# The first transform step of two response chunks, issued behind the next pair's responses

## The chip, the cores and the metric

The kernel runs on one core of a Trainium2 chip. A core has a matrix engine (TensorE, in the profile PE for matmuls and PEld for weight loads), three engines for elementwise work (VectorE = DVE, ScalarE = ACT, GpSimd = POOL), and queues for transfers, of which SyncE's (SP) issues most. The engines work side by side and each takes its own instructions in order. TensorE writes its results to PSUM, which has eight banks per core; the other engines copy them out to SBUF.

The metric is the device time of one execution in microseconds (us), as the median of several runs. Lower is better.

## The reference

The input `x` (2048 rows of 576 columns) is normalised per row. Then three things are summed: `x` itself, a state-space convolution of the normalised rows, and a feed-forward layer (FFN) with SiLU.

```python
xn = _layernorm(x, axis=-1)
# state-space part: 576 channels with 128 modes each give a response K of 2048 steps
P = jnp.exp(logdA[:, :, None] * l[None, None, :])
K = jnp.einsum("dn,dnl,dn->dl", Cc, P, dB).real
...
y = irfft2(rfft2(up) * rfft2(Kp)) + u * Dskip      # causal convolution along 2048 rows
# FFN: 576 -> 4608 -> 576
h = _silu(jnp.einsum("bsd,df->bsf", xn, w1))
out = jnp.einsum("bsf,fd->bsd", h, w2)
return x + y + out
```

## The kernel before

Two streams are woven together. The main one is the FFN: for each of two halves of the rows, nine chunks of hidden columns, two blocks of 512 rows. `up` (lines 313 to 315) makes `ph`, 512 columns wide, from weights and rows split into a high and a low part; `down` (line 338) makes `po`, 288 columns wide, which VectorE adds to the accumulator (line 342). ScalarE and VectorE make `gf`, `gh` and `gl` from `ph` between them (lines 321 to 323).

The side stream is the convolution. Generators yield a position on the FFN's progress, and `weave` runs a side step when the FFN has come that far. The tile framework then orders the instructions of each engine with a schedule that it works out on a modelled timeline; `tc.high_priority()` puts an instruction ahead of others that are ready, and `behind(ins)` places one no earlier than behind the named instruction. So the order in which the code is written is not the order on the engines.

The change lies in `kgen`, which makes the responses. It runs over `NCK` = 36 chunks of 16 channels (8 in each half of the columns). For a chunk, ScalarE and VectorE make tables of sines and cosines `S` and `C` (lines 631 to 654). After each second chunk TensorE multiplies the tables of both:

- `kp` (line 674): 64 small products in each of two terms, with 128 rows and 32 columns of the array each, 64 columns streamed. In the trace each fp32 matmul is two instructions, so that a pair has 128 of them, 2304 in all. `behind(first)` keeps them in one run.
- `kt` (line 681): ScalarE copies the bank `kp` to SBUF.
- `z` (line 689): the first transform step of the response. Eight products with the constant `f1` and 128 columns streamed, each on one half (64 rows) of the array and into its own bank, halves taken in turn; 16 instructions in the trace, 288 in all. Each pair's first product needs `kt`.
- `stage` (line 697): ScalarE copies both banks of `z`, sorted, into a buffer that holds two pairs. When it is full, two transfers bring it to `d1k` in DRAM (line 702), 18 in all.

After the last chunk GpSimd adds the skip row to `d1k` by a transfer (line 705), and `spectral` loads it (`kr`, line 796), splits it (`kh`, `kl`, lines 790 and 791) and multiplies (`pk`, line 804).

Beside `kgen` runs `spread`, which does the same transform step for the normalised rows: `pu` (lines 155 and 156, full array, 288 columns), copied out by ScalarE (line 157, `u`) and sent to DRAM by GpSimd's queue. The two constants `s1` and `f1` come on GpSimd's queue.

`kp`, `z` and `pu` all take their banks from one pool of three, `pss`, in turn: a new tile waits until the tile three before it has been copied out. At the end of the kernel `add_conv` does the last transform step, `py` (line 825), with tiles of 64 rows and 32 columns.

Of the kernel before, what the change touches and what calls it, by code (L numbers as in the profile page):

```python
# [11 lines left out]
F32 = mybir.dt.float32  # L12
# [7 lines left out]
P = 128  # L20
# [23 lines left out]
def kernel(  # L44
# [21 lines left out]
    nc = tc.nc  # L66
# [14 lines left out]
    d1k = dram.tile([32 * P, D], F32, name="d1k")  # L81
# [9 lines left out]
    f1 = cst.tile([P, P], F32, name="f1")  # L91
# [18 lines left out]
    pss = ctx.enter_context(tc.tile_pool(name="pss", bufs=3, space=PSUM))  # L110
# [25 lines left out]
    def behind(ins):  # L136
        return tc.issue_after(ins) if ins is not None else nullcontext()
# [424 lines left out]
    def kgen():  # L562
        fT, phiT = kf["f"], kf["phi"]
        with tc.tile_pool(name="kg", bufs=1) as kg:
            CH = 8
            NRUN = 4
            NCK = HD // CH
# [32 lines left out]
            def powers(i):  # L600

                eb, wb = bases.pop(0)
                load_bases(i + 2)
                nc.scalar.copy(pw[:, :, :, :, 1].rearrange("n q (g c) k -> n q g (c k)", g=2),
                               eb.rearrange("n g q c k -> n q g (c k)"))
                pv = pw.rearrange("n r d k e -> n (r d k) e")
                R = 2 * W * 3
                nc.vector.tensor_mul(pv[:, :, 2], pv[:, :, 1], pv[:, :, 1])
                nc.vector.tensor_mul(pv[:, :, 3:5], pv[:, :, 1:3], pv[:, :, 2:3].broadcast_to([P, R, 2]))
                nc.vector.tensor_mul(pv[:, :, 5:8], pv[:, :, 1:4], pv[:, :, 4:5].broadcast_to([P, R, 3]))  # L610
                return wb

            def head(i):
                th = kg.tile([P, W, 65], F32, tag="th", name="th", bufs=2)
                nc.vector.tensor_mul(split(th), row(vt[:, 0:65], 65), col(fT, i, 65))
                with behind(pins["gl"]):
                    nc.vector.tensor_add(split(th)[:, :, :, :32], split(th)[:, :, :, :32], col(phiT, i, 32))
                return th

            stage = None  # L620
            tabs = []
            nxt = head(0)
            al = powers(0)
            for i in range(NCK):
                th = nxt
                pk, ak = pw[:, i % 2], al[:, :, i % 2]
                c65 = kg.tile([P, W, 65], F32, tag="c65", name="c65")
                S = kg.tile([P, W, 96], F32, tag="S", name="S", bufs=2)
                C = kg.tile([P, W, 96], F32, tag="C", name="C", bufs=2)
                mag = C  # L630
                nc.scalar.activation(c65, th, AF.Identity, bias=magic)  # L631
                nc.vector.scalar_tensor_tensor(th, c65, MAGIC, th, op0=ALU.subtract, op1=ALU.subtract)  # L632
                nc.scalar.activation(c65, th, AF.Abs)  # L633
                nc.scalar.activation(th, th, AF.Sin, scale=TWO_PI)
                nc.scalar.activation(c65, c65, AF.Sin, scale=-TWO_PI, bias=halfpi)
                for g in range(2):
                    gs = slice(g * CH, (g + 1) * CH)
                    nc.vector.tensor_mul(
                        mag[:, gs, 0:32].rearrange("n d (x y) -> n d x y", y=4),
                        pk[:, gs, 0, :].unsqueeze(3).broadcast_to([P, CH, 8, 4]),  # L640
                        ak[:, g].unsqueeze(2).broadcast_to([P, CH, 8, 4]))
                nc.vector.tensor_mul(
                    mag[:, :, 32:96].rearrange("n d (x y) -> n d x y", y=8),
                    pk[:, :, 1, :].unsqueeze(3).broadcast_to([P, W, 8, 8]),
                    pk[:, :, 2, :].unsqueeze(2).broadcast_to([P, W, 8, 8]))
                if i + 1 < NCK:
                    nxt = head(i + 1)
                    if i % 2 == 1:
                        al = powers(i + 1)
                for dst, t, sg in ((S, th, -1.0), (C, c65, 1.0)):  # L650
                    ov3 = dst.rearrange("n d (x y) -> n d x y", y=32)[:, :, 0:3:2, :]
                    mv3 = mag.rearrange("n d (x y) -> n d x y", y=32)[:, :, 0:3:2, :]
                    nc.vector.tensor_mul(ov3, t[:, :, 0:64].rearrange("n d (x y) -> n d x y", y=32), mv3)
                    nc.vector.scalar_tensor_tensor(dst[:, :, 32:64], t[:, :, 64:32:-1], sg, mag[:, :, 32:64],  # L654
                                                   op0=ALU.mult, op1=ALU.mult)
                tabs.append((S, C))
                if i % 2 == 0:
                    yield (i + 1) / NCK
                    continue

                kp = pss.tile([P, 512], F32, tag="pss", name="kp")
                first = None
                for e in (1, 0):
                    S, C = tabs[e]
                    for gl in range(2):
                        for gp_ in range(2):
                            o = e * 256 + (gl * 2 + gp_) * 64
                            for q in range(4):
                                ch = gp_ * CH + gl * 4 + q
                                dst = kp[32 * q:32 * q + 32, o:o + 64]  # L670
                                begins = e == 1 and gl == 0 and gp_ == 0
                                with tc.high_priority(), behind(None if begins else first):
                                    for n, t in enumerate((C, S)):
                                        mm = nc.tensor.matmul(dst, t[:, ch, :32], t[:, ch, 32:],  # L674
                                                              start=begins and n == 0, stop=True,
                                                              tile_position=(0, 32 * q), skip_group_check=True)
                                if begins:
                                    first = mm.ins
                tabs = []
                kt = kg.tile([P, 512], F32, tag="kt", name="kt")  # L680
                nc.scalar.copy(kt, kp)

                z = [pss.tile([P, 512], F32, tag="pss", name="z") for _ in range(2)]
                first = None
                for eg in range(4):
                    for h in (1, 0):
                        rows = slice(64 * h, 64 * h + 64)
                        with tc.high_priority(), behind(first):
                            mm = nc.tensor.matmul(z[h][:, eg * P:(eg + 1) * P], kt[rows, eg * P:(eg + 1) * P], f1[rows],  # L689
                                                  start=True, stop=True, tile_position=(64 * h, 0))  # L690
                        first = first or mm.ins
                r = (i - 1) % NRUN
                if r == 0:
                    stage = kg.tile([P, 64, NRUN * CH], F32, tag="stage", name="stage")
                sv = stage[:, :, r * CH:(r + 2) * CH].rearrange("p k (e h c) -> p h e k c", h=2, c=2)
                for h in range(2):
                    nc.scalar.copy(sv[:, h], z[h].rearrange("p (e k c) -> p e k c", e=4, c=2))
                if r == NRUN - 2:
                    d0 = (i // NRUN) * NRUN * CH
                    kv = d1k.rearrange("(k n) (g d) -> g n k d", n=64, g=2)  # L700
                    for gp_ in range(2):
                        nc.sync.dma_start(kv[gp_, :, :, d0:d0 + NRUN * CH], stage[gp_ * 64:(gp_ + 1) * 64])
                yield (i + 1) / NCK

        nc.gpsimd.dma_start(d1k.rearrange("(k n) d -> n k d", n=P)[0],
# [135 lines left out]
    def side():  # L841
# [3 lines left out]
        with tc.tile_pool(name="kf", bufs=1) as kfp:  # L845
# [50 lines left out]
            with tc.tile_pool(name="up", bufs=1) as up:  # L896
                sp = spread(up)
                for n, at in enumerate(kgen()):
                    if n > 1:
                        next(sp, None)  # L900
                    yield marks[0] + at * (marks[1] - marks[0])
                for _ in sp:
                    pass
# [97 lines left out]
```

## Time and profile before

| | |
|---|---|
| median of 3 runs | 1114.06 us (1113.56 to 1114.08) |
| profiled execution | 1113.42 us, of which its span is 1111.6 us |
| TensorE busy | 1103.3 us (99%), 9168 matmul instructions |
| VectorE busy | 916.9 us (82%) |
| ScalarE busy | 709.2 us (64%) |
| `kp` runs | 18, first start 170.2 us, last 640.2 us into the span |
| `z` runs | 18, first start 177.7 us, last 646.1 us |
| `kt` copies | 18 of 0.572 us (median) |
| `stage` copies | 36 of 0.644 us (median) |

The span runs from the first to the last instruction. In the views below, an instruction's row gives the start and the duration in us, the engine, the line, the operation, the output and the inputs, the tile of the array as rows*columns (only TensorE), the shapes, and how many neighbours of the same kind were merged into the row. A merged row's duration goes from the first one's start to the last one's end. Matmuls are pipelined, so that the next one starts long before the recorded end of the one before; the distance of the starts tells what an instruction costs in the stream.

### The profile page before, as it was taken

Reading aid. Unit: us, or ns where it says so; the run is one execution under the profiler, and the core shown is the slowest. Engines: PE = TensorE matmul, PEld = TensorE weight load, DVE = VectorE, ACT = ScalarE, POOL = GpSimd, SP = SyncE. Lnnn points to the kernel's source line nnn. Section 1 sums busy time; section 2 is a strip of 40 time slices with the busy share of each in tenths; the row PEclk is TensorE's granted clock in tenths of the full one; section 3 lists DMA queues with packets and bytes.
Section 4 is the critical chain, followed back from the end, with each engine's and each line's share of the span. In section 5 each row is a group of like instructions: output and inputs, shape, how many; then the busy total and the mean of one; then the engine's idle time right before and its main releaser. Section 6 shows DMA issues by size and latency. Waiting matters only on the chain.

```text
span 1111.6 us, 22913 instructions
## 1 busy us (share of the span) xinstructions
PE 1103.3 (99%) x9168; PEld 997.8 (90%) x9168; DVE 916.9 (82%) x1546; ACT 709.2 (64%) x1228; POOL 69.8 (6%) x129
## 2 busy tenths in 40 slices
PE   8999999999999999999999999999999999999998
PEld 6998999899889899899989989999999999999887
DVE  6899899999999999999999837787778778784433
ACT  5574456676777676677866536877777878773210
POOL 1100000000000000011000000000000000000111
PEclk9999999999999999999999999999999999999999
DMA  9745522425242515255844163554545445434983
GB/s 258 201 122 152 137 71 61 120 63 130 82 107 80 134 61 131 77 149 161 219 123 105 44 173 106 169 157 128 161 145 150 139 146 171 129 107 130 248 211 86
DMA packets 175563, 148.56 MB, mean 134 GB/s; under 512 B 111024, under 2 KB 142272, under 8 KB 175328
## 3 DMA queue, kind: packets, MB, share of 16 engines
q1 hardware_dynamic: 165136, 112.33, 38.7%
q0 software_dynamic: 9568, 33.62, 9.5%
q8 instruction: 72, 1.18, 0.5%
q10 hardware_dynamic: 752, 1.15, 0.4%
q14 instruction: 35, 0.29, 0.1%
HBM read 102.53 MB, written 44.61 MB: 132 GB/s over the span
## 4 chain that ended last, share of the span: by engine, by line
PE 97%; DMA 1%; DVE 0%; SPq 0%; issue 0%; ACT 0%; ACTq 0%; POOL 0%; DVEq 0%
PE po L338 42%; PE ph L313 35%; PE kp L674 3%; PE ph L314 3%; PE ph L315 3%; PE pu L804 2%; PE pb L804 2%; PE pk L804 2%; PE z L689 2%; PE pu L155 1%; DMA acc<-in_A_u_dram 1%; PE py L825 1%; PE pu L156 1%; DMA w2r<-in_B_w_dram 0%; PE pt L124 0%; DVE st L186 0%
## 5 line engine op out<-in xcount | busy, mean ns | idle before, releaser
L338 PE MATMUL po<-w2l,gh 128*128 128x288 f32 x1152 | 338.5, 295 | 0.9 <-DVE w2l L302 0.9
L338 PE MATMUL po<-w2h,gl 128*128 128x288 f32 x1152 | 336.2, 295 | 0.0
L338 PE MATMUL po<-w2h,gh 128*128 128x288 f32 x1152 | 335.8, 295 | 0.0
L338 PEld LDWEIGHTS po<-w2h,gh 128*128 128x128 f32 x1152 | 215.1, 188 | 7.6 <-issue 2.8
L338 PEld LDWEIGHTS po<-w2l,gh 128*128 128x128 f32 x1152 | 215.9, 188 | 6.1 <-DVE w2l L302 1.1
L338 PEld LDWEIGHTS po<-w2h,gl 128*128 128x128 f32 x1152 | 215.4, 188 | 0.8
L321 ACT ACTIVATE gf<-ph 128x512 f32<-128x512 f32 (+1 forms) x148 | 86.4, 585 | 142.9 <-PE ph L315 128.3
L313 PE MATMUL ph<-xh,w1h 128*128 128x512 f32 (+1 forms) x592 | 162.1, 388 | 1.2 <-ACT gf L321 1.2
L313 PE MATMUL ph<-xl,w1h 128*128 128x512 f32 (+1 forms) x592 | 161.4, 386 | 0.0
L313 PE MATMUL ph<-xh,w1l 128*128 128x512 f32 (+1 forms) x592 | 161.0, 385 | 0.0
L342 DVE TENSOR_TENSOR acc<-po,acc 128x288 f32<-128x288 f32 x288 | 126.4, 452 | 37.4 <-PE po L338 36.1
L323 DVE TENSOR_TENSOR gl<-gf,gh 128x512 fp32r<-128x512 f32 (+1 forms) x148 | 99.2, 673 | 64.8 <-ACT gh L322 64.1
L313 PEld LDWEIGHTS ph<-xh,w1l 128*128 128x128 f32 x592 | 108.1, 188 | 19.9
L313 PEld LDWEIGHTS ph<-xl,w1h 128*128 128x128 f32 x592 | 108.0, 188 | 20.0 <-DVE xl L126 0.2
L313 PEld LDWEIGHTS ph<-xh,w1h 128*128 128x128 f32 x592 | 104.5, 188 | 18.5 <-ACT gf L321 1.8
L322 ACT CAST gh<-gf 128x512 fp32r<-128x512 f32 (+1 forms) x148 | 89.8, 609 | 10.1 <-PE po L338 7.1
L631 ACT ACTIVATE c<-th,magic 128x1040 f32<-128x1040 f32 x36 | 42.1, 1169 | 37.9 <-DVE C L654 28.0
L633 ACT ACTIVATE c<-th 128x1040 f32<-128x1040 f32 x36 | 38.7, 1075 | 34.0 <-DVE th L632 34.0
L300 ACT CAST w2h<-w2r 128x576 fp32r<-128x576 f32 x72 | 46.9, 671 | 17.2 <-PE po L338 14.9
L282 DVE TENSOR_TENSOR w1l<-w1r,w1h 128x640 fp32r<-128x640 f32 x72 | 57.1, 818 | 0.2
L314 PE MATMUL ph<-x,w1h 128*128 128x512 f32 (+1 forms) x148 | 57.0, 385 | 0.0
L315 PE MATMUL ph<-x,w1l 128*128 128x512 f32 (+1 forms) x148 | 56.9, 385 | 0.0
(184 smaller groups left out, 1830.1 us busy)
## 6 DMA issues: line engine op xcount, KB each, us to landing
w2r<-in_B_w_dram SPq DMA_DIRECT2D x72, 288.0 KB, 3.7
w1r<-in_B_w_dram SPq DMA_DIRECT2D x35, 512.0 KB, 3.9
d1u<-u POOLq DMA_DIRECT2D x32, 288.0 KB, 2.6
d1k<-stage SPq DMA_DIRECT2D x18, 512.0 KB, 6.8
ur<-d1u SPq DMA_DIRECT2D x32, 288.0 KB, 3.9
kr<-d1k SPq DMA_DIRECT2D x32, 288.0 KB, 2.8
d<-yo POOLq DMA_DIRECT2D x32, 288.0 KB, 3.7
ys<-d SPq DMA_DIRECT2D x32, 288.0 KB, 11.6
```

The costliest lines, as they stand in the source:

```text
L282: pins["w1l"] = nc.vector.tensor_sub(l1, src, h1).ins
L300: pins["w2h"] = nc.scalar.copy(h2, r2).ins
L313: nc.tensor.matmul(ph, w[:, kt, :], v[:, kt, a:e], start=n + kt == 0, stop=False)
L314: nc.tensor.matmul(ph, h1[:, 4, :], x4[:, a:e], start=False, stop=False)
L315: pins["pe"] = nc.tensor.matmul(ph, l1[:, 4, :], x4[:, a:e], start=False, stop=True).ins
L321: nc.scalar.activation(gf, ph, AF.Silu)
L322: pins["gh"] = nc.scalar.copy(gh, gf).ins
L323: pins["gl"] = nc.vector.tensor_sub(gl, gf, gh).ins
L338: pins["pe"] = nc.tensor.matmul(po[:, :HD], G[blk, t][g][:, js], W2[half, c, t][w][:, hs], start=n == 0, stop=n == 3 * FT - 1).ins
L342: nc.vector.tensor_add(acc[j][:, hs], po[:, :HD], acc[j][:, hs])
L631: nc.scalar.activation(c65, th, AF.Identity, bias=magic)
L804: nc.tensor.matmul(dst, st, mv[:, hs], start=n == 0, stop=n == 3 * len(terms) - 1)
```

## The change

The `z` step of a pair moves out of the loop body into a function `along`. It is no longer issued behind its own pair's `kt`, but behind the next pair's last `kp` matmul (`mm.ins`, passed as `first`), ahead of that pair's `kt` copy. The finished `kt` tiles wait in a list `kts`; so that one can wait while the next is written, `kt` has two buffers. The pair after the last has no responses, so that the last `kt` is transformed right behind its copy, with no instruction to stand behind (`along(None)`; its first `z` then serves as `first` for the others). The copies into `stage` and the transfers to `d1k` move along with `z`. All instructions and their shapes stay.

```diff
             stage = None
+            kts = []
+
+            def along(first):
+                nonlocal stage
+                i, kt = kts.pop(0)
+                z = [pss.tile([P, 512], F32, tag="pss", name="z") for _ in range(2)]
+                for eg in range(4):
+                    for h in (1, 0):
+                        rows = slice(64 * h, 64 * h + 64)
+                        with tc.high_priority(), behind(first):
+                            mm = nc.tensor.matmul(z[h][:, eg * P:(eg + 1) * P], kt[rows, eg * P:(eg + 1) * P], f1[rows],
+                                                  start=True, stop=True, tile_position=(64 * h, 0))
+                        first = first or mm.ins
+                r = (i - 1) % NRUN
...
+                for h in range(2):
+                    nc.scalar.copy(sv[:, h], z[h].rearrange("p (e k c) -> p e k c", e=4, c=2))
+                if r == NRUN - 2:
...
+                        nc.sync.dma_start(kv[gp_, :, :, d0:d0 + NRUN * CH], stage[gp_ * 64:(gp_ + 1) * 64])
...
                 tabs = []
-                kt = kg.tile([P, 512], F32, tag="kt", name="kt")
+                if kts:
+                    along(mm.ins)
+                kt = kg.tile([P, 512], F32, tag="kt", name="kt", bufs=2)
                 nc.scalar.copy(kt, kp)
-
-                z = [pss.tile([P, 512], F32, tag="pss", name="z") for _ in range(2)]
-                first = None
-                for eg in range(4):
...
+                kts.append((i, kt))
+                if i + 1 == NCK:
+                    along(None)
                 yield (i + 1) / NCK
```

More of the change, by code (lines that the diff above doesn't have):

```diff
@@ L620, in kgen @@
             stage = None
+            kts = []
[11 more added lines that the diff above has]
+                r = (i - 1) % NRUN
+                if r == 0:
+                    stage = kg.tile([P, 64, NRUN * CH], F32, tag="stage", name="stage")
+                sv = stage[:, :, r * CH:(r + 2) * CH].rearrange("p k (e h c) -> p h e k c", h=2, c=2)
+                for h in range(2):
+                    nc.scalar.copy(sv[:, h], z[h].rearrange("p (e k c) -> p e k c", e=4, c=2))
+                if r == NRUN - 2:
+                    d0 = (i // NRUN) * NRUN * CH
+                    kv = d1k.rearrange("(k n) (g d) -> g n k d", n=64, g=2)
+                    for gp_ in range(2):
+                        nc.sync.dma_start(kv[gp_, :, :, d0:d0 + NRUN * CH], stage[gp_ * 64:(gp_ + 1) * 64])
             tabs = []
@@ L679, in kgen @@
                 tabs = []
-                kt = kg.tile([P, 512], F32, tag="kt", name="kt")
+                if kts:
+                    along(mm.ins)
+                kt = kg.tile([P, 512], F32, tag="kt", name="kt", bufs=2)
                 nc.scalar.copy(kt, kp)
-                z = [pss.tile([P, 512], F32, tag="pss", name="z") for _ in range(2)]
-                first = None
-                for eg in range(4):
[L686 to L702, printed above, removed]
+                kts.append((i, kt))
+                if i + 1 == NCK:
+                    along(None)
                 yield (i + 1) / NCK
```

## The prediction

> **What bounds the kernel now.** I read the busy times and the chain of waits first, then TensorE's own waits, then the stage that the change touches, and last the order in time at the edges of the two small runs.
>
> ```profile
> PE 1103.3 (99%) x9168; PEld 997.8 (90%) x9168; DVE 916.9 (82%) x1546; ACT 709.2 (64%) x1228; POOL 69.8 (6%) x129
> ...
> PE 97%; DMA 1%; DVE 0%; SPq 0%; issue 0%; ACT 0%; ACTq 0%; POOL 0%; DVEq 0%
> ```
>
> ```profile
> PE pz L857 <- DVE zero L852: 1.3, 1, 1.3
> PE ph L313 <- ACT gf L321: 1.2, 3, 0.5
> PE po L338 <- DVE w2l L302: 0.9, 1, 0.9
> PE pt L124 <- DVE xn L195: 0.2, 1, 0.2
> ```
>
> ```profile
> 165.00:600.00 435.00, 435.00 (x4598) 392.35 (x4598) 422.95 (x632) 305.85 (x463) 19.37 (x35) 1.00 0.42 110
> ```
>
> TensorE carries 97% of the chain and waits 3.6 us for others in the whole run. From 165 to 600 us, where the response chunks are made, it is busy 435.00 of 435.00 us at full clock, and VectorE 422.95 (behind the length stand PE, PEld, DVE, ACT and POOL), so VectorE is the next bound there. On TensorE only two things can change the time: the length of its stream, and a wait that is new. No matmul is added or removed, so the stream changes only by what it costs to pass from one kind of tile to another.
>
> **What an edge costs.** One pair of chunks, in TensorE's order of time (start, duration, count last):
>
> ```profile
> 170.01 0.29 PE L338 MATMUL po<-w2l,gh 128*128 128x288 f32 x1
> 170.23 0.34 PE L674 MATMUL kp<-C 128*32 128x64 f32 x8
> ...
> 171.98 0.31 PE L674 MATMUL kp<-S 128*32 128x64 f32 x6
> 172.22 0.54 PE L338 MATMUL po<-w2h,gl 128*128 128x288 f32 x2
> 172.60 0.29 PE L338 MATMUL po<-w2h,gh 128*128 128x288 f32 x1
> 172.73 0.29 PE L338 MATMUL po<-w2l,gh 128*128 128x288 f32 x1
> ...
> 177.15 0.39 PE L315 MATMUL ph<-x,w1l 128*128 128x512 f32 x1
> 177.37 0.39 PE L313 MATMUL ph<-xh,w1h 128*128 128x512 f32 x1
> 177.69 1.16 PE L689 MATMUL z<-f,kt 64*128 64x128 f32 x16
> 178.78 0.40 PE L155 MATMUL pu<-sp,s 128*128 128x288 f32 x1
> 179.02 0.30 PE L156 MATMUL pu<-sp,s 128*128 128x288 f32 x1
> ```
>
> Full-tile matmuls start 0.13 us apart at 288 columns (172.60 to 172.73) and 0.22 at 512 (177.15 to 177.37). So `kp` was due at 170.14 and starts at 170.23: 0.09 of drain. `z` was due at 177.59 and starts at 177.69: 0.10. Behind a run the first full matmul holds its place for 0.24 instead of 0.13 (178.78 to 179.02), and so do the two `po` at 172.22, which take 0.38 instead of 0.26: 0.11 for weights that could not be loaded ahead. The last `kp` starts at 172.07 (171.98 + 0.31, less the 0.22 that one lasts), 0.15 before the next `po`; the last `z` at 178.58 (177.69 + 1.16, less 0.27), 0.20 before `pu`. The third tile shape, of the last transform step, pays likewise:
>
> ```profile
> 1035.09 1.23 PE L825 MATMUL py<-ys,s 64*32 64x288 f32 x32
> 1036.25 0.40 PE L338 MATMUL po<-w2h,gh 128*128 128x288 f32 x1
> 1036.49 0.29 PE L338 MATMUL po<-w2l,gh 128*128 128x288 f32 x1
> ```
>
> Its last starts at 1035.92, 0.33 before the next, and that one holds its place 0.24. So each change of tile shape costs some 0.09 of drain and 0.11 of exposed load, whichever shapes meet: 0.20. A pair now makes four.
>
> **The change part by part.** In the built order of the changed kernel, 17 of the 18 response runs are followed at once by a `z` run. The first response run stands alone, and the last `z` has no later run to join.
>
> *The joins.* Each takes one full-tile stretch from between two runs: the exposed load behind `kp` (0.11) and the drain ahead of `z` (0.09 to 0.10) go. The drain from `kp` into something else stays, and `z`'s own exposed load is inside its 1.16. 17 x 0.205 = 3.5 us saved. No row shows `kp` beside `z`, so I bound it. If the join costs nothing, the second 0.20 goes as well: 0.40 each, 6.8. If the two shapes need a drain more, 0.10 is left: 1.7. I take 0.205, since three shapes show the same edge.
>
> [...]
>
> *The last `z`.* In the built order it comes in two pieces with six `po` between them: the four matmuls of one 64-row half, then those of the other. Whether halves overlap is seen in three narrow looks at the first run:
>
> ```profile
> 177.69 0.38 PE L689 MATMUL z<-f,kt 64*128 64x128 f32 x2
> 177.69 0.49 PE L689 MATMUL z<-f,kt 64*128 64x128 f32 x4
> 177.69 0.60 PE L689 MATMUL z<-f,kt 64*128 64x128 f32 x6
> ```
>
> Two more instructions, one of each half, add 0.11 together, and the first two start within 0.01: the halves run side by side. A piece of one half (8 instructions) therefore lasts about as long as both. The second piece costs drain 0.10, seven steps of 0.11 and the exposed load (0.88), 0.20 to the next start and 0.11 of load: 1.29 us lost. Its lower bound, if one half alone went twice as fast, is 0.85.
>
> *The later copies, bank and buffers.* The copy `kt` gets a second buffer, because it now waits a pair long for its use; nothing is behind that. The 36 copies into `stage` move to ScalarE's stretch behind `kt`; ScalarE is busy 305.85 of 435, so they cost nothing unless a bank is freed late (rivals). The first `z` of a run now waits for banks that the spread's `pu` held, with the whole FFN stream behind it; in the built order at least 7.4 us of FFN work (matmuls counted at 0.13 and 0.22) stand between the last `pu` and that run, so I cost it at 0. Without that cover it would cost one copy `u` (0.39, line 157 below) a run, 6.6 us.
>
> *The DMAs.* Of the 18 issues of `d1k<-stage`, all but the last two go out a pair later on SP's queue, past up to 20 other issues (weights, tables, `xr`), which they then no longer delay; those behind them wait if ScalarE's copy is late. Only the last pair is followed closely:
>
> ```profile
> 656.93 0.86 POOL L705 DMA_DIRECT2D d1k<-in_A_Dskip_dram  x1 [28.09 <-DMA d1k<-stage]
> 662.76 0.32 SPq L796 DMA_DIRECT2D kr<-d1k  x1
> 673.38 0.67 ACT L790 CAST kh<-kr 128x576 fp32r<-128x576 f32 x1
> 677.75 0.29 PE L804 MATMUL pk<-kh,mm 128*128 128x288 f32 x1
> ```
>
> ```profile
> kr<-d1k SPq DMA_DIRECT2D x32, 288.0 KB, 2.8
> ```
>
> POOL adds the skip row once `stage` has landed, the spectra's first load follows, lands 2.8 us on, and its cast starts 10.6 us after the issue: 7.8 of slack. The built order puts the last `z` behind 1.5 us more FFN work and adds a piece (1.2), so the chain starts 2.7 later: 0. Without that slack it would cost 2.7 once.
>
> *Sum*: 3.5 - 1.3 = 2.2 us off TensorE's stream. The profiled execution took 1113.42 (span 1111.6 and 1.8 around it), which gives 1111.2; the median of the runs, 0.64 above it, gives 1114.06 - 2.2 = 1111.8. About 0.2% (2.2 us) is what a measurement can tell from no change, so the sum lies on that bound.
>
> **Rivals.** *The join costs less.* If drain or load is hidden too, 0.30 a join: 5.1 - 1.3 = 3.8, 1110.3. If nothing is paid, 6.8 - 1.3 = 5.5, 1108.6. For it: `z` loads only halves of the rows, which `kp` might free early. Against: all three shapes pay both parts.
>
> *Slower: the spread's `pu` waits for the bank of `kp`.* Three banks rotate, so `kp` and two `z` take all, and the next `pu` needs `kp`'s, freed by `kt`. ScalarE can be late with that:
>
> ```profile
> 226.93 0.31 PE L674 MATMUL kp<-S 128*32 128x64 f32 x6
> 231.30 0.58 ACT L681 COPY kt<-kp 128x512 f32<-128x512 f32 x1
> ```
>
> ```profile
> 395.35 1.16 ACT L697 COPY stage<-z 128x512 f32<-128x512 f32 x2
> 396.39 0.39 ACT L157 COPY u<-pu 128x288 f32<-128x288 f32 x1
> 396.64 0.30 PE L155 MATMUL pu<-sp,s 128*128 128x288 f32 x1
> ```
>
> That `kt` ended 4.9 us after the last `kp` started (227.02). In the built order the nearest `pu` is nine `po` behind `z`: 0.15 + 0.89 + 0.20 + 0.11 + 8 x 0.13 = 2.4 us behind it. Met together, the wait is 2.5 us; one such in 17 pairs eats the gain (1114.4), and two decide: 5.0 - 2.2 = 2.8 slower, 1116.9. Against: where `pu` stands nine `po` away, `kt` directly follows the cast `c` of line 631, whose input is ready when the tables are; the late one stood behind two sines and three weight casts. Waits for banks exist now and cost nothing, but one was missed narrowly: `pu` at 396.64 takes a bank whose copy, the first of two in 1.16, ended about 0.6 earlier.
>
> *VectorE becomes the bound.* At 422.95 of 435 it may not follow a faster TensorE:
>
> ```profile
> 380.29 0.68 DVE L654 SCALAR_TENSOR_TENSOR C<-c,C 128x512 f32<-128x512 f32 x1
> 382.27 0.26 PE L674 MATMUL kp<-C 128*32 128x64 f32 x2
> ```
>
> Here the tables were ready 1.3 us before `kp` took them. The joins bring TensorE forward by 3.5 in all; past that 1.3, waits of `kp` take up to 2.2 back, and the time is 1114.1. Against: the built order puts `kp` behind up to 4.8 us more FFN work in the middle pairs than now, which widens the slack. That the change does not do what it says is no rival: the 17 joins stand in the built order.
>
> **Chances.** The sum as worked out, within 0.5 us either way: 0.56, a little over half of it (0.30) beyond the bound since a join can more easily be cheaper than shown. A cheaper join: 0.18, all faster. VectorE's bound: 0.09, no change. The bank: 0.17, slower. So faster 0.48, same 0.26 + 0.09 = 0.35, slower 0.17. The forecast is 1111.8; its own range is 1111.3 to 1112.3. Low: 1109.0, between the half-free and the free join (0.03 left out below). High: 1114.6, past VectorE's 1114.1, a single wait for the bank (1114.4) and a join dearer by a drain (1113.7). The bank's cases lie outside: 0.20 left out.
>
> **What would show it.** `kp` to `z` 0.15 from last start to first with `z` still 1.16 long; 17 fewer exposed loads; the last `z` in two pieces of about 1.1 each; no `pu` or `kp` in TensorE's waits. Wrong if the join's gap is near 0.03 or above 0.25, if `pu` waits for `kt` or `stage`, or `kp` for `C`.

## The result and the profile after

The changed kernel takes 1119.53 us (median of 6 runs, 1118.99 to 1121.53), the kernel before, beside it, 1113.87 (6 runs, 1113.51 to 1114.46). The ratio is 1.0058, with a 95% interval of 1.0048 to 1.0069: the change costs 5.7 us, where 2.2 had been forecast as a gain.

The page of the changed kernel: its span, the busy times and, from its fourth part, the chain that ended last.

```profile
span 1117.2 us, 22925 instructions
...
PE 1103.3 (99%) x9168; PEld 999.8 (89%) x9168; DVE 917.4 (82%) x1546; ACT 706.7 (63%) x1228; POOL 70.1 (6%) x129
...
PE 84%; DVE 9%; DMA 2%; ACT 2%; issue 2%; POOL 0%; ACTq 0%; DVEq 0%
```

TensorE is busy as long as before, but carries 84% of the chain instead of 97%; VectorE has 9% of it. The view of TensorE's waits, with the time in us in total, how often, and the longest:

```profile
PE pu L155 <- ACT kt L710: 3.4, 4, 1.2
PE ph L313 <- ACT gf L321: 2.3, 4, 1.1
PE po L338 <- ACT w2h L300: 2.0, 2, 1.7
PE pz L868 <- DVE zero L863: 1.3, 1, 1.3
```

Three of these lines are new or longer, and all that is new lies in the stage of the responses. The window from 165 to 600 us shows it as idle time (behind the length stand PE, PEld, DVE, ACT and POOL):

```profile
165.00:600.00 435.00, 429.37 (x4562) 389.33 (x4561) 418.81 (x626) 301.22 (x458) 19.99 (x36) 1.00 0.42 109
```

TensorE was busy 435.00 of 435 before and is now busy 429.37. The join itself came out as worked out. One response run (64 products, 32 in each of the two terms, so 128 instructions) and the `z` behind it, in TensorE's order of time:

```profile
195.52 0.34 PE L701 MATMUL kp<-C 128*32 128x64 f32 x8
...
197.27 0.31 PE L701 MATMUL kp<-S 128*32 128x64 f32 x6
197.51 1.16 PE L633 MATMUL z<-f,kt 64*128 64x128 f32 x16
198.60 0.40 PE L338 MATMUL po<-w2l,gh 128*128 128x288 f32 x1
198.84 0.30 PE L338 MATMUL po<-w2h,gl 128*128 128x288 f32 x1
```

The last `kp` starts at 197.36 (197.27 + 0.31 - 0.22), the first `z` at 197.51: 0.15. It is the same at all 17 joins. The last `z`, which no run follows, in its two pieces:

```profile
650.23 1.16 PE L633 MATMUL z<-f,kt 64*128 64x128 f32 x8
651.31 0.40 PE L338 MATMUL po<-w2h,gh 128*128 128x288 f32 x1
...
652.30 1.16 PE L633 MATMUL z<-f,kt 64*128 64x128 f32 x8
653.38 0.40 PE L338 MATMUL po<-w2h,gh 128*128 128x288 f32 x1
```

To see where the 5.6 us between the two spans come from, I took the distance from each TensorE instruction's start to the next one's in both traces, less what a full-tile matmul costs in the stream (0.133 us at 288 columns, 0.229 at 512), and added it up by kind:

| where | before | after | difference (us) |
|---|---|---|---|
| drain ahead of small runs | 3.28 (36 times) | 1.80 (20) | -1.5 |
| exposed load behind small runs | 3.83 (36) | 2.10 (20) | -1.7 |
| `kp` to the next, `z` to the next | 6.31 | 6.52 | +0.2 |
| within the `z` runs | 16.02 | 16.90 | +0.9 |
| full matmuls in the stage | -0.96 | 7.85 | +8.8 |
| ahead of the stage | | | -1.1 |
| the sum | | | +5.6 |

The stage is taken from 165 to 720 us. The first four lines are the change of the stream, -2.1. The fifth is nearly all waits: nine distances are over 0.13 us too long, 8.1 us together (0 before): four `pu` that wait for `kt`, 4.05; a `po` at 444.2 and one at 504.2 that wait for `w2h`, 2.35; a `ph` at 639.3 that waits for `gf`, 1.24; two small ones. The sixth is two waits at the start, 0.9 for `w2l` and 0.2 for `xn`, which the new order happens not to have. Below, "waits of the stage" is the sum of the distances that are over 0.13 us too long, from 100 to 720 us of the one profiled execution of each kernel, without what a lower TensorE clock adds (2.1 us in light_a, 0.4 each in spread_even_b and spread_even_late; see the last section).

### The profile page after: what moved, and what is told of

Its sections match the earlier page's. It is cut to its first block, busy times and chain, and to the rows that moved or that the text cites. A ratio compares the mean times of both kernels' runs of the same rounds, so it can differ in the third digit from the quotient of the medians.

```text
span 1117.2 us, 22925 instructions
## 1 busy us (share of the span) xinstructions
PE 1103.3 (99%) x9168; PEld 999.8 (89%) x9168; DVE 917.4 (82%) x1546; ACT 706.7 (63%) x1228; POOL 70.1 (6%) x129
## 4 chain that ended last, share of the span: by engine, by line
PE 84%; DVE 9%; DMA 2%; ACT 2%; issue 2%; POOL 0%; ACTq 0%; DVEq 0%
PE po L338 36%; PE ph L313 30%; PE ph L314 3%; PE ph L315 2%; PE pu L815 2%; PE pb L815 2%; PE pk L815 2%; PE kp L701 2%; DMA w2r<-in_B_w_dram 2%; PE z L633 1%; DVE th L615 1%; DVE C L669 1%; PE py L836 1%; DVE acc L342 1%; DVE S L680 1%
## 5 line engine op out<-in xcount | busy, mean ns | idle before, releaser
L302 DVE TENSOR_TENSOR w2l<-w2r,w2h 128x576 fp32r<-128x576 f32 x72 | 53.6, 750 | 5.0 <-ACT w2h L300 4.9
```

The lines of the kernel that those rows point to most:

```text
L302: nc.vector.tensor_sub(l2, r2, h2)
```

## The experiments

The theories that the expectations name by letters: A, the meeting at the bank of `kp` is the cause and can be cured by itself; the others hold that more is behind it: that the order before is one without slack, so that any new plan of the work draws waits of its own (C), that the joined run itself, whose three banks ScalarE has to empty one behind the other, makes them (D), or that the delay of `z` by a pair does (E).

**The copy ahead of the next chunk's absolute value.** Here is how a `pu` came to wait: the rows of ScalarE at three of the four meetings, in the kernel after, and the `pu` of the first of them (in brackets the idle time ahead of an instruction, and what ended it).

```profile
336.30 1.07 ACT L660 ACTIVATE c<-th 128x1040 f32<-128x1040 f32 x1 [3.84 <-DVE th L659]
337.27 0.57 ACT L710 COPY kt<-kp 128x512 f32<-128x512 f32 x1
...
362.64 1.07 ACT L660 ACTIVATE c<-th 128x1040 f32<-128x1040 f32 x1 [2.71 <-DVE th L659]
...
365.78 0.56 ACT L710 COPY kt<-kp 128x512 f32<-128x512 f32 x1
...
390.64 1.07 ACT L660 ACTIVATE c<-th 128x1040 f32<-128x1040 f32 x1
391.61 0.56 ACT L710 COPY kt<-kp 128x512 f32<-128x512 f32 x1
```

```profile
336.93 0.29 PE L338 MATMUL po<-w2h,gh 128*128 128x288 f32 x1
337.89 0.40 PE L155 MATMUL pu<-sp,s 128*128 128x288 f32 x1 [0.67 <-ACT kt L710]
```

`kp` and the two `z` hold all three banks; `pu` needs that of `kp`, and its copy `kt` stands in ScalarE's order behind the absolute value of the next chunk. At 336 us that one waited 3.84 us for VectorE, and the copy, which needs nothing but `kp`, stood behind it while ScalarE was idle; at 362 us it waited 2.71, and two sines stood ahead of the copy as well; at 390 us, as at the fourth meeting at 506, it did not wait but took its own 1.07 us, behind other work of ScalarE. The edit places that absolute value behind `kt`, in the kernel after (pin) and in the kernel before (before_pin):

```diff
-                nc.scalar.activation(c65, th, AF.Abs)
+                with behind(pins.get("kt")):
+                    nc.scalar.activation(c65, th, AF.Abs)
...
-                nc.scalar.copy(kt, kp)
+                pins["kt"] = nc.scalar.copy(kt, kp).ins
```

> The changed kernel, with the next chunk's absolute value on ScalarE (the one that waits for VectorE's th) placed behind the copy kt. Theory A, the bank: pu waits 3.4 us for kt because kt stands behind that operation; the four waits of pu for kt go, the rest (some 4.3 us for w2h and gf) stays: 1119.5 - 3.4 = 1116.1. Theory B, VectorE is too full and all that it feeds is late: waits move to other places and the time stays at 1118 to 1121.

> The kernel before, with the same operation placed behind kt; z stays a run of its own. A control for what the placing alone does. Theory A: no bank is waited for now, so nothing changes, 1113.5 to 1114.5. Theory B: a new order of the same full engines brings waits of its own, 1115 to 1118.

pin took 1118.46 us (1116.94 to 1122.69), 1.0053 of before (1.0032 to 1.0073); before_pin 1120.58 (1118.63 to 1122.19), 1.0065 (1.0049 to 1.0082). TensorE's waits in pin, as far as they touch the stage, and one at the end of the kernel (`py`):

```profile
PE py L837 <- DMA ys<-d: 1.7, 1, 1.7
PE po L338 <- DVE gl L323: 1.6, 1, 1.6
...
PE po L338 <- ACT w2h L300: 0.5, 1, 0.5
PE pu L155 <- DVE sp L151: 0.4, 1, 0.4
...
PE pu L155 <- ACT kt L711: 0.2, 1, 0.2
```

and the same in before_pin:

```profile
PE po L338 <- ACT w2h L300: 2.8, 2, 2.5
```

The waits for `kt` went from 3.4 to 0.2, so the meeting at the bank is shown to be the cause of those. The waits of the stage fell from 8.1 to 3.8, about as theory A had said. But what is left is mostly not what had been there beside them: a `po` at 232.1 now waits 1.8 for `gl`, and behind the stage `py` waits 1.7 for a transfer. The median, 1118.46, cannot be told from that of the changed kernel. And the same line put into the kernel before, which had no late `kt` to cure, gave it 4.0 us of waits: the edit leaves every instruction as it was and only changes the order. A alone does not carry the result. With about equal waits (3.8 and 4.0) the joined kernel is ahead of the separate one, by 1.7 us in the profiled executions (1116.94 and 1118.63): the shorter stream, 2.1, is seen there.

**Work of VectorE moved to GpSimd.** VectorE was busy 422.95 of 435 us in the stage before. The first product of each chunk's angles goes to GpSimd, in the kernel before (pool_before) and after (pool_after):

```diff
-                nc.vector.tensor_mul(split(th), row(vt[:, 0:65], 65), col(fT, i, 65))
+                nc.gpsimd.tensor_mul(split(th), row(vt[:, 0:65], 65), col(fT, i, 65))
```

> The kernel before, with the first product of each chunk's angles (36 of 1.24 us) moved from VectorE to GpSimd. TensorE waits for nothing in that stretch now, so both theories expect 1113.5 to 1114.5.

> The changed kernel with the same move of 45 us from VectorE to GpSimd. Theory B: the waits of TensorE (7.7 us) go nearly all, and the shorter stream shows: 2.1 us faster than its counterpart with the old order, about 1111.8. Theory A: kt still stands behind operations of the next chunk, so pu's waits of some 3 us stay: 1115 to 1117.

pool_before took 1162.41 us, 1.0441 of before (1.0423 to 1.0459), pool_after 1165.03, 1.0460 (1.0440 to 1.0480); the waits of the stage were some 40 and 42, stretches of lower clock included (granted clock of the two profiled executions 0.993 and 0.988). The groups of instructions from 165 to 650 us (busy time, mean ns of one, idle time ahead) of the kernel before:

```profile
L653 DVE TENSOR_TENSOR C<-c,C 128x1024 f32<-128x1024 f32 x35 | 42.6, 1218 | 0.0
...
L615 DVE TENSOR_TENSOR th<-vt,fT 128x1040 f32<-128x1040 f32 x33 | 40.8, 1236 | 0.1
L654 DVE SCALAR_TENSOR_TENSOR C<-c,C 128x512 f32<-128x512 f32 x35 | 24.0, 686 | 0.1
```

and of pool_before:

```profile
L653 DVE TENSOR_TENSOR C<-c,C 128x1024 f32<-128x1024 f32 x32 | 56.2, 1757 | 0.0
...
L654 DVE SCALAR_TENSOR_TENSOR C<-c,C 128x512 f32<-128x512 f32 x32 | 33.3, 1041 | 0.0
```

```profile
L615 POOL TENSOR_TENSOR th<-vt,fT 128x1040 f32<-128x1040 f32 x32 | 83.3, 2604 | 262.5 <-DVE S L654 238.6 <-ACT stage L697 14.0 <-ACT kt L681 9.9
```

The product takes 2604 ns on GpSimd instead of 1236, and VectorE's products for `C`, which run beside it, went from 1218 to 1757 and from 686 to 1041 ns. So most of what VectorE was spared it lost again, it is still busy 400.50 of the 435 us in pool_before, and the tables come later by the slower product. The pair therefore tells nothing on the question. One thing in it fits the bank: in pool_after, with everything later, `pu` waits for `kt` eleven times:

```profile
PE pu L155 <- ACT kt L710: 15.6, 11, 3.4
```

**More room for the stage.** The side work is told to begin and end at marks of the FFN's progress. With the second mark later, the same responses spread over a longer stretch (the third, for the spectra, moves with it in two of the three). Each was tried with the separate `z` of the kernel before (_b) and the joined one (_a):

```diff
-        marks = (0.13, 0.597, 0.823)
+        marks = (0.13, 0.62, 0.823)    # w62
+        marks = (0.13, 0.64, 0.84)     # w64
+        marks = (0.13, 0.66, 0.84)     # w66
```

> The kernel before, with the response stage woven over more of the FFN (0.13 to 0.64 of its progress instead of 0.597, the spectral stage to 0.84): the same work of VectorE in a stretch 9% longer. Theory B (VectorE too full): no waits of TensorE in the stage, about 1113.9. Theory C (the order before happens to be free of waits, and any other plan brings some): 1115 to 1120.

> The changed kernel with the same longer stage. Its stream has the same 17 joins and the same last z in two pieces. Theory B: waits of TensorE fall from 7.7 to under 1 us, and it is 2.1 us faster than its counterpart with separate runs, 1111.8. Theory A (kt behind the next chunk's operations): pu's waits of some 3 us stay, 1115. Theory C: some other waits, a time 2 us below its counterpart on the mean but with several us either way.

> The kernel before with the stage to 0.66 (13% longer). Theory B: no waits in the stage, 1113.9. Theory C: 1115 to 1120.

> The changed kernel with the stage to 0.66. Theory B: 1111.8, without waits in the stage. Theory A: 1115, with waits of pu for kt. Theory C: anything between 1112 and 1118.

> The kernel before with the response stage woven to 0.62 of the FFN's progress instead of 0.597, the rest of the marks as they are. Waits in the stage 0 to 4 us as in the other separate forms (Theory C and D alike).

> The changed kernel with the stage to 0.62. Theory C (a lottery of plans, joined or not): waits in the stage as in its counterpart, and a time 2.1 us below it. Theory D: 2 to 5 us more waits than its counterpart, and no gain over it.

| | us | ratio to before (95%) | waits of the stage |
|---|---|---|---|
| w62_b | 1121.45 | 1.0065 (1.0040 to 1.0089) | 0 |
| w62_a | 1118.78 | 1.0062 (1.0038 to 1.0085) | 2.1 |
| w64_b | 1136.21 | 1.0207 (1.0193 to 1.0221) | 1.0 |
| w64_a | 1141.54 | 1.0238 (1.0219 to 1.0258) | 3.4 |
| w66_b | 1149.07 | 1.0312 (1.0290 to 1.0333) | 1.5 |
| w66_a | 1149.38 | 1.0327 (1.0312 to 1.0341) | 4.2 |

As times these say little on the change: the later mark pushes the spectra into the end of the kernel, and there it is paid for. In w64_b TensorE is busy 24.63 of the 40 us from 1040 on, at a granted clock of 0.74, and one `ph` waits 9.1 us:

```profile
1040.00:1080.00 40.00, 24.63 (x148) 20.04 (x147) 10.41 (x20) 6.63 (x14) 3.05 (x6) 0.74 0.76 182
```

```profile
PE ph L313 <- ACT w1h L280: 9.1, 1, 9.1
```

Within the stage they do say something: at each mark the joined kernel waits 2.1 to 2.7 us longer than the separate one, which is as much as its stream is shorter. In w62 the stage gains nothing by that sum: 2.1 saved, 2.1 waited. (The medians have w62_a 2.7 us ahead, but the two ranges, 1117.96 to 1124.77 and 1116.99 to 1123.02, cover each other.)

**The spread's steps elsewhere.** The `pu` that meet `kp`'s bank come from `spread`, one step per chunk. Here both steps of a pair stand behind the even chunk, away from the run, with the separate `z` (spread_even_b), the joined one (spread_even_a), and the joined one with the edit of pin as well (spread_even_pin):

```diff
-                    if n > 1:
+                    for _ in range(2 if n > 1 and n % 2 == 0 else 0):
                         next(sp, None)
```

> The changed kernel, with both steps of the spread for a pair issued behind the even chunk, none behind the pair's joined run. In the built order the first pu now stands 12 to 36 po behind the joined run, mostly over 20, where it was 9 to 24. Theory A (the bank): pu waits for kt nowhere, TensorE's waits in the stage fall from 8.1 us to 4 or less, 1115.5. Theory C (any new order of these full engines brings waits, joined or not): 2 to 6 us of waits at other places, 1114 to 1118, and as many in its counterpart.

> The kernel before with the same move of the spread's steps: z a run of its own. Theory A: no waits in the stage, 1113.9. Theory C: 1 to 4 us of waits, 1115 to 1118.

> The changed kernel with both cures at once: the spread's steps behind the even chunk, and the next chunk's absolute value behind kt, so that no pu stands near a bank that is late. Theory A: waits in the stage under 2 us, 1112 to 1114. Theory C or D: no pu waits, but 3 to 8 us at other places, 1116 to 1121.

spread_even_a took 1125.64 us, 1.0107 (1.0092 to 1.0122); spread_even_b 1120.47, 1.0065 (1.0050 to 1.0080); spread_even_pin 1120.11, 1.0064 (1.0042 to 1.0086). The waits of the stage were 8.8, 2.9 and 4.1. In spread_even_a no `pu` waits for `kt` any more, and this stands in its place:

```profile
PE po L338 <- ACT w2h L300: 4.6, 2, 3.3
PE po L338 <- DVE acc L342: 2.0, 1, 2.0
```

So with the meeting gone, the joined kernel waits as long as the changed one, for other things. Both cures together leave 4.1.

**Less work for VectorE.** light_a and light_b leave out the addition of the phase to the angles, so that VectorE has one instruction a chunk less:

```diff
-                with behind(pins["gl"]):
-                    nc.vector.tensor_add(split(th)[:, :, :, :32], split(th)[:, :, :, :32], col(phiT, i, 32))
```

> The changed kernel with the addition of the phase to the angles left out (36 operations of 0.69 us on VectorE, so that the responses lack their phase). In the built order six z runs stand apart in halves, so that the stream saves only 16 x 0.2 - 5 x 1.2 or so: it is some 2 us longer than before. Theory B (VectorE too full): waits in the stage below 1 us, 1116. Theory C: 2 to 6 us of waits, 1118 to 1122.

> The kernel before with the same addition left out. Theory B: no waits, 1113.9. Theory C: 1 to 4 us of waits, 1115 to 1118.

light_a took 1122.59 us, 1.0084 (1.0069 to 1.0099), light_b 1119.02, 1.0048 (1.0031 to 1.0064); the waits of the stage were 5.6 and 4.4. The kernel before has none. Taking work from the fullest engine of the feeders, which also gave a new order, brought 4.4 us of waits: some more room on VectorE (410.35 of 435 us busy in light_b) does not by itself keep them away.

**The step of its own, not joined.** `z` is issued in the code in the middle of the next pair, with no instruction to stand behind, at the three placings for which the separate and the joined kernel had been seen:

```diff
                 if i % 2 == 0:
+                    if kts:
+                        along(None)
                     yield (i + 1) / NCK
...
-                if kts:
-                    along(mm.ins)
```

> z still comes a pair late, but as a run of its own, behind the next even chunk: the deferral without the join. In the built order it has 21 z runs (three in halves), all apart from kp, so that the stream is 3 x 1.3 = 3.9 us longer than before. Theory D (the waits come from the join: three banks are full at once, and ScalarE must empty them in one go): waits in the stage like those of the separate forms, 0 to 4 us, so 1118 to 1121. Theory E (they come from z being a pair late): 6 us or more, 1123 and up.

> Side work placed a little later (mark 0.62), and the transform step a pair late as a run of its own, not joined: the third kernel at this placing, beside the separate one (no new wait of TensorE in the stage) and the joined one (2.1 us of waits). Theory D (the meeting of response run and transform run itself brings the waits, since three banks then have to be emptied at once): waits in the stage 0 to 1 us, though the step is a pair late as in the joined kernel. Theory C (each plan of the work has its own few waits, drawn blindly): 0 to 4 us, as likely above 2 as below. The time by D is 1118 to 1122, since some twenty pieces of the small run cost about 5 us of stream more than the 18 of before; by C the same plus the waits.

> The spread's two steps behind the even chunk, and the transform step a pair late as a run of its own, not joined: the third kernel at this placing, beside the separate one (3.3 us of waits in the stage) and the joined one (8.8 us). Theory D: about what the separate kernel has, 2 to 4 us, and well below the joined one. Theory C: anywhere from 0 to 9 us. If it has 7 us or more, lateness by itself brings the waits here and D falls for this placing. The time by D is 1120 to 1124.

late_apart took 1121.19 us, 1.0067 (1.0045 to 1.0089); w62_late 1124.63, 1.0106 (1.0083 to 1.0129); spread_even_late 1119.46, 1.0058 (1.0037 to 1.0079). The waits of the stage were 0.35, 0 and 3.2. But the edit missed its purpose: the framework put `z`, which has high priority, 4.9 to 5.5 us behind its `kp` on the mean, as before (5.1), and not 26.8 as in the changed kernel. So the expectations' "a pair late", and with it theory E, was not tried. What the three are is three more plans with a separate `z`. Two of them are dearer by their stream: in late_apart the 18 `z` runs became 21 pieces, some of one half alone, which costs 5.1 us by the same adding up as above, and in w62_late 20; in spread_even_late they stayed 18.

**What they show together.** The waits of the stage, separate and joined at the same placing:

| | separate | joined |
|---|---|---|
| as in the diff | 0 | 8.1 |
| pin | 4.0 | 3.8 |
| w62 | 0 | 2.1 |
| w64 | 1.0 | 3.4 |
| w66 | 1.5 | 4.2 |
| spread_even | 2.9 | 8.8 |
| light | 4.4 | 5.6 |
| the mean | 2.0 | 5.1 |

With the three apart (0.35, 0, 3.2), and the two of GpSimd left aside, ten separate plans have 1.7 us on the mean, from 0 to 4.4; with spread_even_pin eight joined ones have 5.0, from 2.1 to 8.8. Both theories keep a part. A plan of its own costs something (C): the kernel before has no wait at all, and six of the nine other separate plans have about one microsecond or more. And the joined plans wait longer (D): in six of seven pairs 1.2 to 8.1 us more, 3.2 on the mean of all seven, against 2.1 that the stream becomes shorter in all but light (there `z` falls into halves). That is a tendency of a few plans with one trace each. By their medians two joined kernels are ahead of their counterparts (pin by 2.1 us, w62 by 2.7) and five behind (by 0.3 to 5.7), and only in the diff's own pair, spread_even and light do the ranges stand apart.

What the waits are for differs. In the separate plans 13.3 of the 17.3 us are `po` that wait for `w2h`, the FFN's second weights. ScalarE casts them when their transfer `w2r` has landed; here are its waits for that, from 165 to 650 us, in the kernel before and in spread_even_b:

```profile
ACT w2h L300 <- DMA w2r<-in_B_w_dram: 2.1, 3, 1.7
```

```profile
ACT w2h L300 <- DMA w2r<-in_B_w_dram: 15.5, 7, 4.9
```

In the nine other separate plans this is 4.2 to 16.6 us. The changed kernel, with 10.6, shows how the `po` at 444 came to wait:

```profile
441.17 0.99 SPq L291 DMA_DIRECT2D w2r<-in_B_w_dram  x2
```

```profile
445.49 0.67 ACT L300 CAST w2h<-w2r 128x576 fp32r<-128x576 f32 x1 [1.27 <-DMA w2r<-in_B_w_dram]
```

The issue at 441.17 was released at 441.16 by VectorE's `w2l` (there are two buffers of `w2r`), the transfer landed at 445.46, and the cast followed. So what a new order costs here is mostly that these weights come late; no kernel was tried that asks for them earlier or gives them more buffers. The joined plans wait as long for `w2h` (1.6 us on the mean of eight, against 1.3 of ten). What they have more is 1.2 us for `kt` and 2.2, against 0.4, for other things (`gl`, `gf`, `gh`, `w1h`, `acc`, a bank of `u`). Whether the meeting of the two runs or the delay of `z` by a pair brings those last ones stays open: no kernel had the one without the other.

## Why the prediction was wrong

- *The joins*: right. 0.15 from `kp` to `z` was foretold and is there; drain (0.09) and load (0.106) saved 17 x 0.196 = 3.3 us, for which 3.5 had been taken. The last `kp` stands 0.15 us ahead of `z` at the joins (197.36 to 197.51), as it stood ahead of a full tile before (172.07 to 172.22), while within the run it is 0.058 from one `kp` to the next in the same 32 columns (197.36 less 195.52, for 127 steps on four column tiles; an estimate); so some 0.09 of the 0.15 comes with the new shape, from small to small as from small to full. "Drain" is the author's name for this gap; what TensorE does in it no run shows. Neither the cheaper join nor a dearer one came.
- *The last `z`*: right. Two pieces of 1.16 cost 1.3 (0.9 within the runs, 0.4 at the edges); 1.29 had been taken, not the lower 0.85.
- *The stream in sum*: -2.1 for -2.2.
- *The copies and the banks*: this is the step that failed. "They cost nothing unless a bank is freed late" set the sum's term for waits at 0 and left the rest to a rival of 0.17. Four `pu` met the late copy, 4.05 us. Met together a wait was worked out at 2.5, from the latest copy seen (4.9 us behind the last `kp`) and the nearest `pu` (nine `po` behind `z`). The four `pu` that met it stand 16 to 23 `po` behind `z`, and their copies ended 4.2 to 5.7 us behind the last `kp`: 0.6 to 1.4 each, but more of them than the "two" that were to decide it.
- Within it, the argument against that rival looked at one place only: "where `pu` stands nine `po` away, `kt` directly follows the cast `c` of line 631". At such a place it came true (line 658 in the changed kernel), the copy ended at 416.01 and the `pu` at 416.15 had no wait:

```profile
414.37 1.17 ACT L658 ACTIVATE c<-th,magic 128x1040 f32<-128x1040 f32 x1 [0.91 <-DVE th L617]
415.45 0.57 ACT L710 COPY kt<-kp 128x512 f32<-128x512 f32 x1
```

- But a copy 4.9 us late also reaches a `pu` some 27 `po` away (4.9 less 1.35 for `z` and its edges, at 0.13 each), and those were not gone through. In the changed kernel `kt` stands there behind the absolute value of line 660, which at 336.30 and 362.64 waited for VectorE's `th`. The order was read at the nearest `pu` and not at each one within reach, nor as far as what the copy's neighbour waits for itself.
- *The other half of the waits*, 4.1 us for `w2h`, `gf` and others, had no term and no rival. The 2.35 for `w2h` go back to late transfers; where the rest comes from is open. The prediction asked which wait the change makes at the places that it touches. It took for granted that a plan made anew would be as free of waits everywhere else as the one before, which from 165 to 600 us had none; of the others only w62_b and w62_late had none in the stage.
- *VectorE as the bound*: not seen. No `kp` waits for `C`, and VectorE is less busy (418.81 of 435). *The first `z`'s bank* and *the last pair's chain of DMAs*, costed at 0, cost 0: neither stands in the waits. (In light_a the first one did come: a `z` waited 1.9 us for the copy `u`.)
- The sum with what was measured: 1113.42 - 2.1 + 8.8 - 1.1 = 1119.0, the profiled execution's own 1118.99.

## What to carry to other kernels

Where the bound engine runs without a wait and a scheduler weaves the others around it, that order is itself worth something: an edit that moves instructions gets a new order, and a forecast should carry a term for its waits, here 0 to 4 us for the separate plans and 2 to 9 for the joined ones, before it counts a gain of 2. When a tile takes the last bank of a rotating pool, go through every user of the pool that a late copy can reach, not only the nearest, and read on the copying engine not only what stands ahead of the copy but what that instruction waits for. And joining two runs that fill the banks of one pool brings the next user of the pool closer to the copy that frees it: the `pu` that came 4.6 us or more behind the last `kp` before came as little as 2.5 behind that of a joined run after.

## What the runs showed of the hardware

**Behind two waits the clock was halved.** In light_a a `z` waited 1.9 us for a bank. Then this followed (the number behind the engines' columns is the granted clock):

```profile
452.00:455.00 3.00, 1.14 (x6) 0.90 (x6) 1.21 (x2) 3.00 (x6) 0.00 (x0) 0.88 0.00 0
455.00:458.00 3.00, 3.00 (x13) 2.78 (x13) 3.00 (x6) 2.12 (x5) 0.00 (x0) 0.50 0.10 23
458.00:461.00 3.00, 3.00 (x8) 2.32 (x8) 3.00 (x5) 1.37 (x3) 0.54 (x1) 0.50 0.33 108
461.00:464.00 3.00, 3.00 (x15) 2.23 (x15) 2.94 (x6) 0.60 (x1) 0.00 (x0) 0.98 0.66 207
```

Half the clock (0.50) for 6.8 us (by windows of half a microsecond from 454.3 to 461.1), in which a row of four `ph` took 1.91 us (from 457.70) instead of 1.08 (from 638.14 in the changed kernel, at a clock of 1.00). In spread_even_late, behind a wait of 3.0 us at 444 (the waits here as in the view of TensorE's waits), it was 3.4 us, from 448.1 to 451.5:

```profile
449.00:451.00 2.00, 2.00 (x8) 1.81 (x8) 2.00 (x3) 0.01 (x1) 0.00 (x0) 0.50 0.50 146
```

In the profiled executions of spread_even_b and spread_even_a, with longest waits of 2.7 and 3.3 us, the granted clock was 0.998 and 0.997 on the mean. In the changed kernel a wait of 1.7 us at 444 had no such sequel (1.00 from 444 to 456), and neither had one of 1.8 in w66_a (1.00 from 500 to 720) and one of 2.5 in before_pin (1.000 over the whole execution). So the length of a wait does not tell here whether half the clock follows: behind 1.9 us it did in light_a, behind 2.5 it did not in before_pin. What sets it off no run shows.

A lower granted clock also goes with longer times: the five executions of w62_a had spans of 1116.2 to 1117.0 us at a mean granted clock of 0.998 to 1.000, and of 1120.6 and 1123.0 at 0.996 and 0.997, while all of the kernel before were at 0.999 or 1.000. How much of those 4 to 6 us the clock makes is open. In the profiled one, of 1123.0 us, it was 0.83 from 1080 to 1090; over the whole, 0.003 of 1123.0 below full is worth some 3.4 us (an estimate), and `py` waited 5.6 for transfers.
